# Decode attention on one core: results turned by fp32 transpositions, bias of both halves in one product

## The chip, the core and the metric

One core of one Trainium2 chip. The time is device microseconds of one execution, read off the chip. Each execution also has a profile with a span, from the first to the last instruction that is recorded; the time is about 2 us longer than the span. Kernels are compared with runs of the kernel before made on the same chip in the same session. Ratios are the mean time of one kernel's fast runs over the mean of the other's fast runs of the same rounds, so they are not quite the ratio of the medians quoted here. In the lines of the profile PE is TensorE, PEld its weight loads, DVE VectorE, ACT ScalarE, POOL GpSimd and SP SyncE, which issues the loads; a q behind such a name is that engine's sequencer, and L237 is line 237 of the kernel.

## The reference, cut to what matters

```python
# x: (2, 1, 448); k_cache, v_cache: (2, 8, 32768, 256), the last W = 4096 positions are used
xn = layernorm(x)
q  = xn @ wq                                   # 16 heads of 256; 2 query heads share a key head
p  = softmax(q @ k.T * 256**-0.5)              # over 4096 positions
A  = (p @ v).reshape(2, 1, 4096) @ wo
h  = xn @ w1 + b1                              # 448 -> 1792
B  = (h * tanh(softplus(h))) @ w2              # 1792 -> 448
return x + A + B
```

All inputs are bf16. The keys and values of the window alone are 2 x 2 x 8 x 4096 x 256 elements of 2 bytes, 67 MB, and every byte is used once.

## The kernel before

The eight key heads go round one after the other: a key load of 4 MB, a value load of 4 MB and a piece of the output weights, all on one DMA queue; VectorE transposes the keys, TensorE makes the scores, ScalarE their exponentials, VectorE transposes those, and TensorE multiplies them with the values. The first six key heads end like this: `values` leaves an 8 x 512 result (2 groups of keys x 4 rows of batch and head), ScalarE copies it, `turn_o` turns it so that the key dimension lies on the partitions and adds the two groups, `finish` scales it and keeps each partition's own head, `mix` multiplies with the output weights.

```python
def turn_o(i):
    o_sb = state.pop(("o", i))
    pq = ps_q.tile([P, NJ * BR], FP32, tag="q", name="q")          # NJ = 4, BR = 4
    ...
    for j in range(NJ):
        for u in range(NP):                                        # NP = 2 groups of keys
            nc.tensor.matmul(pqv[:, j, :],
                lhsT=o_sb[:, u, j, :, :]..., rhs=ident_f[0:NR, u * BR : (u + 1) * BR],
                start=(u == 0 and j == 0), stop=(u == NP - 1), ...)

def finish(i):       # o = pq * (1/sum);  o = o * own;  oT = o[head 0] + o[head 1]
    ...
def dense_in():
    for c in range(NF):                                            # NF = 7
        for s in range(NS):                                        # NS = 7
            nc.tensor.matmul(hT_ps[:, c, :, :], lhsT=w1_v[:, s, c, :], rhs=xs[:, s, :, :],
                             start=(s == 0), stop=False, ...)
        for x in range(NX):                                        # NX = 2 halves of the layer
            nc.tensor.matmul(hT_ps[:, c, x, :], lhsT=b1_v[:, x, c, :], rhs=ones[:, :], ...)
```

The last two key heads take another way (`values_fixed`): their result comes out turned already, and sixteen small products with the output weights close the program.

The softmax here doesn't subtract the row's maximum and nothing guards it: scores larger than these inputs give would overflow.

## Time and profile before

| | before |
|---|---|
| time, median of 3 runs | 190.53 us (190.34 to 190.56) |
| span of the profiled run | 188.1 us (time 190.5) |
| TensorE, VectorE, ScalarE busy | 148.5, 106.8, 45.3 us |
| DMA | 77.66 MB, 96.7% of the span |
| last packet of an input, from the packet records | 184.20 us |
| store of the result issued | 185.88 us |

### The profile page before, as it was taken

The numbers are of one execution on the slowest core, as the hardware profiler recorded it, in microseconds if no ns is written. First come the engines' busy times: TensorE is split into PE (matmuls) and PEld (weight loads), VectorE is DVE, ScalarE is ACT, GpSimd is POOL, SyncE is SP. The second block draws the span as 40 slices with busy tenths as digits, with TensorE's granted clock in tenths as the row PEclk, the third lists the DMA queues.
The fourth block names the chain that finished last, engine by engine and source line by source line (L and its number), as shares of the span: only waits on it lengthen the run. The fifth ranks groups of instructions, "written<-read, shape, count | busy, mean of one in ns | idle before, by whom it ended". The sixth has DMA issues, their size and how long they took to land.

```text
span 188.1 us, 2516 instructions
## 1 busy us (share of the span) xinstructions
PE 148.5 (79%) x993; PEld 73.3 (39%) x993; DVE 106.8 (57%) x144; ACT 45.3 (24%) x148; POOL 16.4 (9%) x74
## 2 busy tenths in 40 slices
PE   0493099904989999978995989958995989999782
PEld 0141033901334454425342624334442534355771
DVE  6505497049671994089704991099407984985201
ACT  3005015200062225123322224032402242234001
POOL 7001500300003001200030003000110000000000
PEclk9999559965899999999999999999999999999955
DMA  6999899999999999999999999999999999999990
GB/s 223 422 470 446 378 441 428 439 442 446 432 446 439 427 407 414 432 432 405 473 430 439 439 432 425 418 432 421 440 439 439 400 429 432 456 432 390 425 367 17
DMA packets 5028, 77.81 MB, mean 414 GB/s; under 512 B 533, under 2 KB 1049, under 8 KB 2330
## 3 DMA queue, kind: packets, MB, share of 16 engines
q1 hardware_dynamic: 5012, 77.66, 96.7%
q8 instruction: 7, 0.11, 0.2%
q14 instruction: 3, 0.02, 0.0%
q10 hardware_dynamic: 6, 0.01, 0.0%
HBM read 77.67 MB, written 0.00 MB: 413 GB/s over the span
## 4 chain that ended last, share of the span: by engine, by line
DMA 67%; DVE 21%; PE 7%; SPq 1%; issue 1%; ACT 1%; ACTq 0%; DVEq 0%
DMA k<-in_A_k_cache_dram 57%; DVE kt L404 17%; DMA v<-in_A_v_cache_dram 10%; PE o L477 4%; DVE pT L442 3%; PE sc L416 3%; SPq L373 1%; ACT p L430 1%; PE psA L237 0%; SPq L114 0%; DVE sums L451 0%; DVE osum L536 0%; DVE oTm L543 0%; PE q L559 0%; ACTq L663 0%
## 5 line engine op out<-in xcount | busy, mean ns | idle before, releaser
L404 DVE STREAM_TRANSPOSE kt<-k 128x2048 f32<-128x2048 f32 x32 | 73.1, 2289 | 52.7 <-DMA k<-in_A_k_cache_dram 52.7
L416 PE MATMUL sc<-kt,qdiag 128*128 128x512 bf16 x256 | 62.5, 389 | 17.4 <-DVE kt L404 16.7
L430 ACT ACTIVATE p<-sc,off 128x256 bf16<-128x256 f32 x64 | 33.0, 543 | 70.7 <-PE sc L416 70.1
L416 PEld LDWEIGHTS <-qdiag 128*128 128x128 bf16 x256 | 23.0, 97 | 52.8 <-issue 20.5
L477 PE MATMUL o<-v,pT 128*8 128x512 bf16 x192 | 42.5, 379 | 0.0
L477 PEld LDWEIGHTS <-pT 128*8 128x8 bf16 x192 | 17.2, 92 | 22.4
L442 DVE STREAM_TRANSPOSE pT<-p 128x512 bf16<-128x512 bf16 x32 | 21.8, 682 | 5.5 <-ACT p L430 5.5
L289 POOL COPY qdiag<-qt 32x16 bf16<-32x16 bf16 x64 | 12.9, 247 | 120.2 <-PE sc L416 104.6
L486 ACT COPY o_sb<-o 8x512 f32<-8x512 f32 x12 | 6.3, 572 | 36.3 <-PE o L477 36.3
L516 PEld LDWEIGHTS q<-ident_f,o_sb 8*128 8x128 f32 x96 | 11.1, 186 | 2.5 <-issue 2.5
L430 ACT ACTIVATION_READ_ACCUMULATOR p<-sc,off 128x1 f32 x64 | 11.7, 182 | 0.0
L516 PE MATMUL q<-ident_f,o_sb 8*128 8x4 f32 x96 | 11.7, 249 | 0.0
L220 PE MATMUL psE<-v,act_bf 128*2 128x448 bf16 x14 | 4.8, 528 | 6.8 <-DVE act_bf L354 6.8
L269 PE MATMUL q_ps<-v,xq 128*128 128x512 bf16 x28 | 7.8, 446 | 2.5 <-DMA v<-in_A_wq_dram 2.5
L559 PE MATMUL q<-pT,v 128*128 128x4 bf16 x256 | 7.9, 169 | 1.5 <-DMA v<-in_A_v_cache_dram 1.3
L559 PEld LDWEIGHTS <-v 128*128 128x128 bf16 x256 | 7.5, 100 | 2.3 <-DMA v<-in_A_v_cache_dram 1.8
L220 PE MATMUL psE<-wo,oTm 128*2 128x448 bf16 x24 | 5.5, 352 | 2.9 <-DVE oTm L543 2.9
L269 PEld LDWEIGHTS <-xq 128*128 128x128 bf16 x28 | 3.1, 112 | 7.1 <-DVE xq L260 2.5
L279 DVE CAST q_sb<-q_ps 128x512 bf16<-128x512 f32 x2 | 1.3, 686 | 7.7 <-PE q_ps L269 7.7
L220 PEld LDWEIGHTS <-act_bf 128*2 128x2 bf16 x14 | 1.5, 116 | 9.8 <-DVE act_bf L354 6.9
L220 PEld LDWEIGHTS <-oTm 128*2 128x2 bf16 x24 | 1.5, 82 | 7.0 <-DVE oTm L543 4.9
L190 PE MATMUL xnT_ps<-ident,xn_bf 2*128 2x2 bf16 x7 | 0.5, 166 | 4.6 <-DVE xn_bf L138 4.6
(60 smaller groups left out, 44.2 us busy)
## 6 DMA issues: line engine op xcount, KB each, us to landing
k<-in_A_k_cache_dram SPq DMA_DIRECT2D x7, 4096.0 KB, 27.2
v<-in_A_v_cache_dram SPq DMA_DIRECT2D x7, 4096.0 KB, 29.4
k<-in_A_k_cache_dram SPq DMA_DIRECT2D x2, 2048.0 KB, 24.5
v<-in_B_w_dram SPq DMA_DIRECT2D x2, 1568.0 KB, 24.4
wo<-in_A_wo_dram SPq DMA_DIRECT2D x7, 448.0 KB, 30.4
v<-in_A_wq_dram SPq DMA_DIRECT2D x1, 2048.0 KB, 7.4
v<-in_A_v_cache_dram SPq DMA_DIRECT2D x1, 2048.0 KB, 15.4
v<-in_A_wq_dram SPq DMA_DIRECT2D x1, 1536.0 KB
```

The lines of the kernel that those rows point to most:

```text
L220: nc.tensor.matmul(psE[:], lhsT=lhsT, rhs=w, start=start, stop=stop, skip_group_check=True)
L269: nc.tensor.matmul(ps[u][:], lhsT=xq[:, s, :, :].rearrange("p j k -> p (j k)"), rhs=wq_sb[:, s, u * N5 : (u + 1) * N5], start=(s == 0), st ...
L289: nc.gpsimd.tensor_copy(out=tv[rows, :, e, j * Q : (j + 1) * Q : HS].rearrange("p n (b h) -> p n b h", b=Bsz), in_=qv[rows, :, h0 : h0 + r ...
L373: nc.sync.dma_start(out=t[:, cols], in_=src[:, :, cols])
L404: nc.vector.transpose(out=kt[:].bitcast(FP32), in_=k[:, half * TH * Dh : (half + 1) * TH * Dh].bitcast(FP32),)
L416: nc.tensor.matmul(psc[:], lhsT=qdiag[i % NW][:, n * NE + e, :], rhs=ktv[:, n, e, :, :], start=(n == 0 and e == 0), stop=(n == NB - 1 and ...
L430: nc.scalar.activation(out=pv[:, b, :, :], in_=sv[:, b, :, :], func=ACT.Exp, scale=scale, bias=off[:, b : b + 1], accum_out=state["rs", i] ...
L442: nc.vector.transpose(out=pT[:], in_=p_t.pop(s)[:])
L477: nc.tensor.matmul(po[:], lhsT=pT_t[i * NH + piece][:, uh * NP * Q : (uh + 1) * NP * Q : HS], rhs=v[:, u * NP : (u + 1) * NP, :].rearrange ...
L486: nc.scalar.copy(out=o_sb[:, u, :, :, :], in_=po[:, u * Dh : (u + 1) * Dh] .rearrange("r (m j) -> r j m", j=NJ) .unsqueeze(2) .to_broadcas ...
L516: nc.tensor.matmul(pqv[:, j, :], lhsT=o_sb[:, u, j, :, :].rearrange("r h m -> r (h m)"), rhs=ident_f[0:NR, u * BR : (u + 1) * BR], start=( ...
L559: nc.tensor.matmul(po[:, c, :], lhsT=vv[:, t, c, :], rhs=pTv[:, th, 0:Q:HS], start=(t == 0 and c == 0), stop=(t == T - 1), skip_group_chec ...
```

## The change

Its intent: fewer and cheaper TensorE instructions. An fp32 product of the kernel before shows as two records in the trace (96 for 48 products); the hope is that an fp32 transposition shows as one. So `turn_o` only transposes, and the two groups of keys and the two heads are added on VectorE afterwards. The VectorE sums need more on-chip memory; the bias in two rows instead of one takes 1.8 KB a partition less, and with it the bias of both halves becomes one product with a small identity.

```diff
-    b1_sb = consts.tile([1, F], BF16)
+    b1_sb = consts.tile([NX, HF], BF16)          # loaded as two rows
+    half = consts.tile([NX, NX, Bsz], BF16)      # copied from the identity
...
-            for x in range(NX):
-                nc.tensor.matmul(hT_ps[:, c, x, :], lhsT=b1_v[:, x, c, :], rhs=ones[:, :], ...)
+            nc.tensor.matmul(hT_ps[:, c, :, :]..., lhsT=b1_v[:, c, :], rhs=half[:]..., ...)
...
-        state["rec", i] = denominator(i)
+        rec = denominator(i)                     # and rec * own into state["rec", i], on VectorE
...
-                nc.tensor.matmul(pqv[:, j, :], lhsT=o_sb[:, u, j, :, :]...,
-                    rhs=ident_f[0:NR, u * BR : (u + 1) * BR], ...)
+                nc.tensor.transpose(pqv[:, j, u, :], o_sb[:, u, j, :, :]..., ident_f[0:NR, 0:NR])
...
-        o = pq * rec;  o = o * own;  oT = o[..., 0] + o[..., 1]         # three VectorE operations
+        for u in range(NP): o[:, :, u, :] = pqv[:, :, u, u * BR : (u + 1) * BR] * rec
+        oT = tensor_reduce(o over u and h)                               # three VectorE operations
```

More of the change, by code (lines that the diff above doesn't have):

```diff
@@ L100 @@
     nc.scalar.dma_start(out=x_bf[:, :], in_=A_x.flatten_outer_dims())
-    b1_sb = consts.tile([1, F], BF16)
-    nc.scalar.dma_start(out=b1_sb[:, :], in_=B_b1.rearrange("(o f) -> o f", o=1))
+    b1_sb = consts.tile([NX, HF], BF16)
+    nc.scalar.dma_start(out=b1_sb[:, :], in_=B_b1.rearrange("(x f) -> x f", x=NX))
     def v_tile():
@@ L212 @@
             )
-    ones = consts.tile([1, Bsz], BF16)
-    nc.vector.memset(ones[:], 1.0)
     psE = ps_a.tile([Bsz, D], FP32, name="psE")
@@ L296, in build_q @@
                 )
+    half = consts.tile([NX, NX, Bsz], BF16)
+    nc.vector.tensor_copy(
+        out=half[:], in_=ident[0:NX, 0:NX].unsqueeze(2).to_broadcast([NX, NX, Bsz])
+    )
     act_bf = consts.tile([P, NF, NX, Bsz], BF16)
@@ L317, in dense_in @@
         w1_v = dense.pop("w1").rearrange("p s (q c) -> p s c q", c=NF)
-        b1_v = b1_sb[:].rearrange("o (x q c) -> o x c q", x=NX, c=NF)
+        b1_v = b1_sb[:].rearrange("x (q c) -> x c q", c=NF)
         hT_ps = ps_m.tile([P, NF, NX, Bsz], FP32, tag="m", name="hT_ps")
@@ L329, in dense_in @@
                 )
-            for x in range(NX):
-                nc.tensor.matmul(
-                    hT_ps[:, c, x, :],
-                    lhsT=b1_v[:, x, c, :],
-                    rhs=ones[:, :],
-                    start=False,
-                    stop=True,
-                    skip_group_check=True,
-                )
+            nc.tensor.matmul(
+                hT_ps[:, c, :, :].rearrange("p x b -> p (x b)"),
+                lhsT=b1_v[:, c, :],
+                rhs=half[:].rearrange("o x b -> o (x b)"),
+                start=False,
+                stop=True,
+                skip_group_check=True,
+            )
         shape = [P, NF, NX, Bsz]
@@ L473, in values @@
         v = v_t.pop(i)
-        state["rec", i] = denominator(i)
+        rec = denominator(i)
+        state["rec", i] = small.tile([P, BR], FP32, tag="recm", name="recm")
+        nc.vector.tensor_tensor(
+            out=state["rec", i][:],
+            in0=rec[:],
+            in1=own[:].rearrange("p b h -> p (b h)"),
+            op=ALU.mult,
+        )
         for u in range(T // NP):
@@ L511, in turn_o @@
         o_sb = state.pop(("o", i))
-        pq = ps_q.tile([P, NJ * BR], FP32, tag="q", name="q")
-        pqv = pq[:].rearrange("p (j r) -> p j r", j=NJ)
+        pq = ps_q.tile([P, NJ * NP * NR], FP32, tag="q", name="q")
+        pqv = pq[:].rearrange("p (j u r) -> p j u r", j=NJ, u=NP)
         for j in range(NJ):
             for u in range(NP):
-                nc.tensor.matmul(
-                    pqv[:, j, :],
-                    lhsT=o_sb[:, u, j, :, :].rearrange("r h m -> r (h m)"),
-                    rhs=ident_f[0:NR, u * BR : (u + 1) * BR],
-                    start=(u == 0 and j == 0),
-                    stop=(u == NP - 1),
-                    skip_group_check=True,
+                nc.tensor.transpose(
+                    pqv[:, j, u, :],
+                    o_sb[:, u, j, :, :].rearrange("r h m -> r (h m)"),
+                    ident_f[0:NR, 0:NR],
                 )
@@ L528, in finish @@
         rec = state.pop(("rec", i))
-        o = small.tile([P, NJ, Bsz, rep], FP32, tag="osum", name="osum")
-        nc.vector.tensor_tensor(
-            out=o[:].rearrange("p j b h -> p j (b h)"),
-            in0=pqv,
-            in1=rec[:].unsqueeze(1).to_broadcast([P, NJ, BR]),
-            op=ALU.mult,
-        )
-        nc.vector.tensor_tensor(
-            out=o[:].rearrange("p j b h -> p j (b h)"),
-            in0=o[:].rearrange("p j b h -> p j (b h)"),
-            in1=own[:].rearrange("p b h -> p (b h)").unsqueeze(1).to_broadcast([P, NJ, BR]),
-            op=ALU.mult,
-        )
-        oT = small.tile([P, NJ, Bsz], BF16, tag="oTm", name="oTm")
-        nc.vector.tensor_tensor(
-            out=oT[:], in0=o[:, :, :, 0], in1=o[:, :, :, 1], op=ALU.add
-        )
+        o = small.tile([P, NJ, NP, BR], FP32, tag="osum", name="osum")
+        for u in range(NP):
+            nc.vector.tensor_tensor(
+                out=o[:, :, u, :],
+                in0=pqv[:, :, u, u * BR : (u + 1) * BR],
+                in1=rec[:].unsqueeze(1).to_broadcast([P, NJ, BR]),
+                op=ALU.mult,
+            )
+        oT = small.tile([P, NJ, Bsz], BF16, tag="oTm", name="oTm")
+        with nc.allow_low_precision("sums of fp32 factors, rounded once"):
+            nc.vector.tensor_reduce(
+                out=oT[:],
+                in_=o[:].rearrange("p j u (b h) -> p j b u h", b=Bsz),
+                axis=AXIS.XY,
+                op=ALU.add,
+            )
         state["oT", i] = oT
```

## The prediction

What no trace or run of this case shows of the hardware is cut from the recorded text, and the cuts are marked. Its sum: TensorE 142.0 us, VectorE 108.0 us and 0.0 us on the path that sets the end, so 190.5 us. A "pass" in it is one record of the trace, two for each fp32 product. In the third rival, that an idle stretch brings the clock down was the author's assumption, from one stretch in which it fell (idle from 37.9 to 44.8 us) beside one in which it did not (2.1 us); in the range, the allowance for another chip's rate was a guess.

> **What bounds the kernel now.** I read the page from the top: span and engines, the row of slices, the DMA queues, the chain. Then the queue's own waits, one-microsecond and longer windows, and the timeline of the end.
>
> ```profile
> span 188.1 us, 2516 instructions
> PE 148.5 (79%) x993; PEld 73.3 (39%) x993; DVE 106.8 (57%) x144; ACT 45.3 (24%) x148; POOL 16.4 (9%) x74
> ...
> DMA  6999899999999999999999999999999999999990
> ...
> q1 hardware_dynamic: 5012, 77.66, 96.7%
> ...
> DMA 67%; DVE 21%; PE 7%; SPq 1%; issue 1%; ACT 1%; ACTq 0%; DVEq 0%
> ```
>
> The reader is to see that no compute engine is near its span (TensorE 79%, VectorE 57%), while one DMA queue is at work for 96.7% of it, in every slice but the first and the last. 77.66 MB pass through it, and the change moves none of those bytes. The windows say how steadily:
>
> ```profile
> 0.00:4.00 4.00, 0.00 (x0) 0.00 (x0) 2.23 (x6) 1.58 (x2) 3.39 (x10) 1.00 0.60 193
> 4.00:60.00 56.00, 37.22 (x190) 17.38 (x191) 28.81 (x44) 11.17 (x36) 6.45 (x33) 0.82 1.02 435
> 60.00:120.00 60.00, 54.48 (x271) 25.50 (x270) 36.15 (x42) 16.01 (x54) 4.90 (x24) 1.00 1.00 430
> 120.00:180.00 60.00, 52.80 (x436) 27.23 (x434) 38.74 (x49) 16.03 (x54) 1.64 (x8) 0.99 1.00 426
> ```
>
> Columns: stretch, length, busy time and count of PE, PEld, DVE, ACT, POOL, the granted TensorE clock, DMA share, GB/s. The transfer rate is 435, 430 and 426 GB/s in three stretches in which TensorE's load differs much (37 of 56 us, then 54 of 60). The span is therefore a sum: 1.65 us of start-up, then bytes over rate, then the tail after the last byte.
>
> The chain of waits seems to say otherwise, because it gives VectorE 21%: each key load is "released" by the VectorE transposition that frees its buffer. So the second question is whether the queue ever runs dry. The queue's own waits:
>
> ```profile
> SPq L373 <- PE o L477: 53.8, 6, 11.1
> SPq L373 <- DVE kt L404: 50.2, 6, 10.2
> ...
> SPq L373 <- PE psE L220: 17.6, 1, 17.6
> ```
>
> The sequencer that issues loads does wait on TensorE and VectorE, for over 100 us. To see what that costs I added up the GB/s of 188 one-microsecond windows and set the sum against the megabytes issued so far. When a load is issued, this much is still queued ahead of it: 3.6 MB at the value load at 49.63 us (the one behind the 17.6 us wait), 5.7 to 7.7 MB at all loads from 55 to 143 us, and 3.6 MB at the last value load at 163.01 us. At 428 GB/s the smallest of these is 8.4 us of work, the usual one 17 us. So the waits are waits for a free buffer ahead of a full queue; they hold back no byte until a release comes more than 8 us later than today.
>
> The end:
>
> ```profile
> 164.89 18.50 DMA v<-in_A_v_cache_dram
> 183.40 0.05 issue
> 183.44 0.39 PE q L559 x8
> 183.83 0.02 issue
> 183.86 0.18 DVE oT L498
> ```
>
> The last bytes land at 183.40 us. What follows, 4.7 us, is eight value products, a scaling, sixteen products of the output projection, two copies and the store. All of it belongs to the last two key heads, which go through another routine (values times weights directly transposed) that the diff does not touch.
>
> [...] here, from 60 to 170 us, the one-microsecond windows with VectorE above 0.9 average 432 GB/s and those below 0.1 average 431. So fewer or more engine operations should not change the rate. [...] no fp32 transposition is in this trace, so its duration is the uncertain one below. [...] idle from 37.9 to 44.8 us the clock fell to 0.5, while the idle of 2.1 us before the score products at 144.7 us left it at 1.00.
>
> **The change part by part.**
>
> (1) Turning the results of six key heads (the fp32 products at L516). Now, for one head:
>
> ```profile
> 164.75 1.86 PEld L516 LDWEIGHTS q<-ident_f,o_sb 8*128 8x128 f32 x16 [0.42 <-issue]
> 164.76 1.94 PE L516 MATMUL q<-ident_f,o_sb 8*128 8x4 f32 x16
> ```
>
> Eight products are recorded as 16 (two passes each) and take 1.94 us, that is 0.117 us a pass once pipelined. After, eight transpositions of 8x128 with an identity of 8 columns. If each is one pass: 8 x 0.117 = 0.94 us plus the last one's 0.1, so about 1.0 us, 0.9 us less a head and 5.6 us less over six heads. If each still takes two passes: nothing saved. Nothing waits for TensorE's time there beyond a microsecond: in that head the next score products (L416) start at 166.63 us, and TensorE then runs on to the final value products.
>
> (2) VectorE's sums. Now a head has three operations, 0.135 + 0.176 + 0.167 = 0.48 us. After: a product of reciprocals with the head mask, on 128x4 (the row nearest to it, the mask product of 128x16, takes 0.176; I take 0.15), two products of 128x16 from PSUM (0.135 each at the least, 0.176 when waiting), and a reduction of 128x32 to 128x8 (the reduction of 128x8 takes 0.120, the sum 0.167; I take 0.2). Sum 0.15 + 0.31 + 0.20 = 0.66, that is 0.18 us more a head and about 1.1 us over six heads. These sit in VectorE's chain between the key transpositions, so each key load's issue moves about 0.2 us later, against 17 us of queued work: no effect on landing.
>
> (3) The bias of the dense layer. 14 products become 7; from the timeline a pair took 0.26 us, so seven pairs become seven singles and 0.9 us goes from TensorE around 33 to 38 us. The VectorE copy that consumes them (L341) starts only at 43.1 us, because it stands behind the next key transpositions on its engine, so the gain ends as idle time. The bias load becomes two rows of 1.8 KB in place of one of 3.5 KB; it has 30 us to land. A memset of 0.06 us becomes a small copy of some 0.14 us in the start, where the first projection waits for it and for the query weights alike: at most 0.1 us.
>
> Sum by engine: TensorE 148.5 - 5.6 - 0.9 = 142.0 us, VectorE 106.8 + 1.1 + 0.1 = 108.0 us, DMA bytes unchanged. On the path that sets the end, start-up plus bytes over rate plus tail: 0.0 us, give or take 0.1. So 190.5 us.
>
> **The rivals.** First: the buffers' releases matter after all, through TensorE. In the last part TensorE is busy without a break from 156 to 177 us, and the final value load at 163.01 us is released by its value products. If the queue were dry, 0.9 us less a head would shift that load, and the time would fall by 1 to 2 us (to about 189). Against it: 3.6 MB are queued at that moment, and the DMA share is 1.00 up to 180 us. The value products are also gated by VectorE's fourth key transposition (ending at 153.82, the scores at 153.96), not by the turned results.
>
> Second: the extra VectorE work lengthens the chain that the page prints. If a chain of "VectorE transposition, key load" really set the pace, 0.2 us a head over six heads would add 1.2 us (191.7). Against it is the same queue: a key load takes 25 to 29 us to land although 4 MB need only 9.8 us.
>
> Third: the clock. With less to do, TensorE idles longer[...]. The steady round is 20.4 us with 17.4 us of TensorE; at half clock for a whole round, the matrix products of 512 columns would take (from the 0.43 us spacing seen at clock 0.50) some 27 us, and TensorE would become the bound: 200 us or more if it stuck. Against it: the long idle stretch in a round waits for a key load, between value products and the first score products, and the freed time falls elsewhere, just behind those first score products, in pieces of about 1 us. A dip at the end, where the clock is 0.5 from 179 us already, changes nothing as the products there wait for data.
>
> Fourth: the transfers run at another rate because of a different chip or placement[...].
>
> **Range and chances.** The three runs of before span 0.22 us. To that I add 0.2 us for the start and the reordering and some for another chip's rate: 189.9 to 191.1 us holds it 8 times in 10. Two per cent is 3.8 us. A gain of that size would need DMA time to vanish, and no byte does: 1%. A loss needs the third rival or a start-up stall: 2%. The rest, 97%, is within 2%.
>
> **What would show it.** Right: the DMA queue again near 97% with 77.66 MB, about 430 GB/s in the three stretches, last value landing near 183.4 us and 4.7 us after it; L516's successor with 48 records in place of 96 and about 1.0 us a head; TensorE near 142 us and VectorE near 108 us. Wrong in a part: 96 records for the transpositions (two passes), or VectorE's new operations well above 0.66 us a head; neither would move the time. Wrong in the whole: a stretch in the steady part with a DMA share well under 1, a granted clock of 0.5 between 60 and 170 us, or a load landing later with TensorE or VectorE named as its releaser and nothing queued ahead.

## The result, and the profile after

The changed kernel takes 189.66 us (median of 6 runs, 189.53 to 190.00) against 190.55 us of before (6 runs, 190.34 to 190.63). The ratio of the fast runs is 0.9957 (95% interval 0.9944 to 0.9969). That is 0.9 us less: small, well inside the 2% band, but clear of the noise and below the range (189.9 to 191.1).

The page of the changed kernel, its lines for the span, the engines, the slices, the queue and the chain:

```profile
span 187.8 us, 2412 instructions
PE 141.0 (75%) x938; PEld 65.0 (35%) x938; DVE 108.6 (58%) x150; ACT 45.3 (24%) x148; POOL 16.3 (9%) x74
...
q1 hardware_dynamic: 5012, 77.66, 96.9%
...
DMA 66%; DVE 20%; PE 8%; SPq 2%; ACT 1%; issue 1%; ACTq 0%; DVEq 0%
```

TensorE does 7.5 us less, VectorE 1.8 us more, and the DMA queue the same bytes. The same three windows as before (columns as in the prediction):

```profile
4.00:60.00 56.00, 37.44 (x186) 17.20 (x187) 29.46 (x49) 11.46 (x37) 6.42 (x33) 0.85 1.01 434
60.00:120.00 60.00, 50.48 (x245) 21.33 (x244) 36.50 (x45) 16.02 (x54) 4.90 (x24) 1.00 1.00 430
120.00:180.00 60.00, 49.31 (x418) 23.39 (x416) 39.06 (x52) 16.03 (x54) 1.63 (x8) 0.98 1.00 427
```

434, 430 and 427 GB/s: the transfers run as they did. Added up microsecond by microsecond, the two kernels' bytes agree within 0.1 MB from 179 us on, and the last packet of an input lies at 184.20 us before and 184.26 us after. So none of the 0.9 us comes from ahead of the last byte. The turning of one head, in the timeline of the changed kernel:

```profile
165.06 0.57 PEld L523 LDWEIGHTS q<-ident_f,o_sb 8*128 8x128 f32 x8 [0.42 <-issue]
165.06 0.66 PE L523 MATMUL q<-ident_f,o_sb 8*128 8x8 f32 x8
```

One record for each transposition instead of two for each product, and 0.66 us instead of 1.94. The freed time went where the prediction said: into TensorE's waits. Its product and weight-load tracks together now wait 16.8 us for VectorE's sums (7.8 before).

What did change is the tail. First the chain of waits of the kernel before, from where the prediction broke off (start, length, what):

```profile
184.08 0.35 PE psA L237 x6
184.43 0.44 issue
184.86 0.49 PE psA L237 x10
185.35 0.23 ACT res L635
```

Sixteen like products: six, then a hole of 0.44 us labelled "issue" (the engine waits for nothing that the profile shows), then ten. There is a real wait in these sixteen, for the last weights, but it stands ahead of the ninth product, not of the seventh. The same place in the changed kernel, by weight loads (start, length, engine, ..., count):

```profile
184.15 0.18 PEld L234 LDWEIGHTS <-oT 128*2 128x2 bf16 x9 [0.35 <-DVE oT L505]
184.58 0.10 PEld L234 LDWEIGHTS <-oT 128*2 128x2 bf16 x7 [0.26 <-issue]
```

Here the pause stands where it belongs: nine weight loads and eight products go, the ninth product starts at 184.58, right after the last weights land at 184.54, as the chain of the changed kernel has it:

```profile
167.20 17.34 DMA wo<-in_A_wo_dram
184.54 0.04 issue
184.58 0.46 PE psA L234 x8
```

Before, even the seventh and the eighth product, whose weights had landed at 183.96 us, started only at 184.86. But the hole cost less than its length. The trace also records the sixteen completion signals of that load: the last of them came at 184.71 us before, 0.50 us behind the last packet, and at 184.54 us after, 0.27 us behind it. In the six traces without a hole in which the ninth product waits for that signal, it starts 0.04 to 0.05 us behind it. So before it could have started at about 184.75 us instead of 184.87, and the hole cost about 0.12 us there (an estimate from these figures; the store follows the start of the ninth product by 1.01 us in both kernels). From the last packet to the store it is 1.68 us before (185.88 - 184.20) and 1.33 us after (185.59 - 184.26). Of this 0.35 us the later signal is 0.23 us and the hole 0.12 us; what delayed the signal, no run tells. Since the last packet lies 0.06 us later in the changed kernel, the spans differ by 0.3 us. The rest of the 0.9 us is outside them: 190.5 - 188.1 = 2.4 us before, and in the six runs of the changed kernel 1.81 to 1.88 five times and 2.3 once.

### The profile page after: what moved, and what is told of

Its sections match the earlier page's. It is cut to its first block, busy times and chain, and to the rows that moved or that the text cites. A ratio compares the mean times of both kernels' runs of the same rounds, so it can differ in the third digit from the quotient of the medians.

```text
span 187.8 us, 2412 instructions
## 1 busy us (share of the span) xinstructions
PE 141.0 (75%) x938; PEld 65.0 (35%) x938; DVE 108.6 (58%) x150; ACT 45.3 (24%) x148; POOL 16.3 (9%) x74
## 3 DMA queue, kind: packets, MB, share of 16 engines
q1 hardware_dynamic: 5012, 77.66, 96.9%
## 4 chain that ended last, share of the span: by engine, by line
DMA 66%; DVE 20%; PE 8%; SPq 2%; ACT 1%; issue 1%; ACTq 0%; DVEq 0%
DMA k<-in_A_k_cache_dram 57%; DVE kt L404 16%; DMA wo<-in_A_wo_dram 9%; PE sc L416 4%; PE o L484 4%; DVE pT L442 3%; SPq L373 2%; ACT p L430 1%; PE psE L217 0%; SPq L114 0%; DVE sums L451 0%; SPq L398 0%; DVE oTm L544 0%; DVE recm L476 0%; PE psA L234 0%
## 5 line engine op out<-in xcount | busy, mean ns | idle before, releaser
L266 PE MATMUL q_ps<-v,xq 128*128 128x512 bf16 x28 | 8.7, 487 | 2.1 <-DVE xq L257 2.1
L523 PEld LDWEIGHTS q<-ident_f,o_sb 8*128 8x128 f32 x48 | 3.4, 136 | 2.5 <-issue 2.5
L276 ACT CAST q_sb<-q_ps 128x512 bf16<-128x512 f32 x2 | 1.1, 588 | 12.5 <-PE q_ps L266 12.5
```

The costliest lines, as they stand in the source:

```text
L266: nc.tensor.matmul(ps[u][:], lhsT=xq[:, s, :, :].rearrange("p j k -> p (j k)"), rhs=wq_sb[:, s, u * N5 : (u + 1) * N5], start=(s == 0), st ...
L523: nc.tensor.transpose(pqv[:, j, u, :], o_sb[:, u, j, :, :].rearrange("r h m -> r (h m)"), ident_f[0:NR, 0:NR],)
```

## The experiments

Twelve kernels, five rounds each, in three sets; the runs of before made with them have a median of 190.58, 190.51 and 190.58 us. In each set one or two of the eleven runs of before took 192.4 to 192.8 us; they are under the bound for the slow state and so are in the ratios, which is why I quote medians, and spans and times outside them for each run. Because of those slow runs the 95% interval of the ratio reaches 1 for five of the twelve kernels (`after_pad`, `before_pad24`, `after_pad55`, `turn_pad48`, `after_pad44`); what is said of them rests on medians and ranges. All twelve kernels gave the right result.

### First set: which half of the change, and is it the length of TensorE's program?

The trace of before has an 8 KB instruction fetch 2.1 us after its span, that of after has none. That made my first theory: the shorter program saves a fetch. Rivals: the saved work itself, or the other form of the bias load.

`bias_only`: the bias half of the diff on the kernel before, nothing else.

> The kernel before with the bias half of the change alone (14 fewer TensorE instructions, a two-row bias load, nothing else). Program-length theory (an instruction fetch of 8 KB that the trace of before shows 2.1 us after its span, and that of after lacks, is paid in the time): 189.7 to 190.0 us, no such late fetch, time less span near 1.9 us instead of 2.4. Work theory (the shorter turning of results on TensorE makes the gain): 190.5 us. Bias-load theory (the two-row load or the changed start makes it): 189.7 us.

`turn_only`: the other half on the kernel before.

```diff
 # the changed kernel with the bias as before, and, to fit:
-        o = small.tile([P, NJ, NP, BR], FP32, tag="osum", name="osum")
+        o = small.tile([P, NJ, NP, BR], FP32, tag="osum", name="osum", bufs=2)
```

> The turning half alone (transpositions and VectorE sums), bias as before; one small tile has two buffers instead of three because it does not fit otherwise. As many TensorE instructions in the program as before. Program-length theory: 190.2 to 190.5 us, the late fetch is there. Work theory: 189.7 us. Bias-load theory: 190.5 us.

`after_pad`: the changed kernel with seven products issued twice (the first of each group, which only overwrites itself).

```diff
-            for s in range(NS):
+            for s in (0, *range(NS)):
```

> The changed kernel with seven bias-layer products issued a second time (same result), so that TensorE's program has as many instructions as before: 14 more than after. Program-length theory: back to 190.2 to 190.5 us, the late fetch returns. Work theory and bias-load theory: 189.7 us.

`after_again`: the changed kernel as it is.

> The changed kernel once more, as the control of this set: 189.7 us against 190.5 us of before under every theory; if it is 190.2 or more, the 0.9 us was a matter of the chip or the load and no theory is needed.

| | time, median (range) | span, median | outside the span, six runs | last packet to store |
|---|---|---|---|---|
| before | 190.58 | 188.3 | 2.17 to 2.46 (eleven runs) | 1.68 us |
| bias_only | 189.99 (189.86 to 190.18) | 188.05 | 1.79 to 1.88, one 2.18 | 1.55 us |
| turn_only | 189.90 (189.64 to 190.32) | 187.8 | four 1.82 to 1.89, two 2.3 | 1.34 us |
| after_pad | 190.09 (189.70 to 190.47) | 187.95 | two 1.8, four 2.29 to 2.37 | 1.32 us |
| after_again | 189.88 (189.58 to 190.43) | 187.9 | three 1.8 to 1.9, three 2.2 to 2.3 | 1.32 us |

(The last column is from each one's trace.) Ratios: 0.9960, 0.9956, 0.9963, 0.9957. So the 0.9 us is not a matter of the chip, but either half alone brings 0.6 to 0.7 us of it, and they do not add. The theory of program length had `bias_only` right (189.7 to 190.0 us, no late fetch), but it fell: the padded kernel, though its trace has the late fetch again, came to 190.09 us and not back to 190.2 or more; the turning half, which I had counted as no shorter, was as fast as the whole, and the late fetch shows in the unchanged `after_again` (2.07 us after its span). The theory of the bias load fell with the turning half, which keeps the old load and is as fast. The work theory fell in that the bias half, which saves 0.4 us of TensorE's time (seven groups of products at 0.61 us instead of 0.66) at a place where nothing waits for it, brought most of the gain.

What remained was the hole in the tail. The weight loads of `bias_only`:

```profile
184.14 0.18 PEld L234 LDWEIGHTS <-oT 128*2 128x2 bf16 x9 [0.35 <-DVE oT L498]
184.59 0.09 PEld L234 LDWEIGHTS <-oT 128*2 128x2 bf16 x4 [0.28 <-issue]
184.94 0.09 PEld L234 LDWEIGHTS <-oT 128*2 128x2 bf16 x3 [0.26 <-issue]
```

Behind the regular pause at the ninth there is a second one, after 13 of the 16: seven products later than in before, and seven products (each a weight load and a product, so 14 instructions) are what the bias half removes. Counted from the last product backwards, the hole lies 20 instructions from the end in before and 6 in `bias_only`. In both, the same kind of hole lies 256 instructions earlier: 276 from the end in before (after 8 of 64 products at 178.48 us), 262 in `bias_only` (after 15). The four kernels with the turning half, 96 recorded instructions shorter or more, have none in the last 32.

So the second theory: TensorE's instruction stream is cut every 256 instructions, the distance between the two holes of one kernel (276 - 20 in before, 262 - 6 in `bias_only`), and at a cut TensorE can stand still (0.44 us in before). That it waits there for instructions is a guess that no run shows; the page's queue list has seven packets of 16 KB of the kind "instruction" in before, after, `bias_only` and `turn_only`, and no more than that. Where no hole is found, the place of a cut is computed from the 256 and the instructions that were added. The line of the page (queue, kind, packets, MB, share):

```profile
q8 instruction: 7, 0.11, 0.2%
```

### Second set: move the cut, not the work

All four kernels add needless products at the start of the bias layer (they overwrite themselves, the result is the same), after 33 us and before 50 us, far from the tail:

```diff
-            for s in range(NS):
+            for s in [0] * k + list(range(NS)):    # k for each of the 7 groups, n in all
```

`before_pad24`: n = 24 in the kernel before.

> The kernel before with 24 needless products (48 TensorE instructions) in the bias layer, same result. Boundary theory (TensorE's instruction stream is cut every 256 instructions; in before a cut lies 20 instructions from the end of the products, inside the last 16 products after the last byte, and costs some 0.35 us there; in the first set the cut lay at 6 in the bias half, and at none in the last 32 of the others): the cut moves to 68 from the end, where TensorE waits for data anyway, so no unexplained gap in the last 16 products, store issued 1.33 us after the last packet instead of 1.68, span about 187.9, although TensorE does more work than in before. Work theory (less TensorE work makes the gain): span 188.2 or more, store 1.68 us after the last packet.

`after_pad55`: n = 55 in the changed kernel.

> The changed kernel with 55 needless products, which makes up exactly the 110 TensorE instructions that the change removed. Boundary theory: the cut is again 20 from the end; TensorE stalls after six of the last 16 products until about 184.85, store 1.6 to 1.7 us after the last packet, span 188.2 as before, 0.35 us over the changed kernel. Work theory: about 4 us of TensorE work come back near 40 us, not in the tail; the span stays at 187.85 or, if any work counts, goes back to 188.2 too, but without a stall after six products.

`after_pad51`: n = 51.

> The changed kernel with 51 needless products, four fewer than the one above. Boundary theory: the stall moves by four products, to ten of the last 16 done (12 instructions from the end), store 1.5 to 1.7 us after the last packet, span 188.0 to 188.2. Work theory: no stall at a definite place, span as with 55.

`after_pad79`: n = 79.

> The changed kernel with 79 needless products, more than the one with 55: as many TensorE instructions as the padded before. Boundary theory: cut at 68 from the end, no stall in the last 16 products, store 1.33 us after the last packet, span 187.85: more work and yet 0.35 us faster than with 55. Work theory: as slow as with 55 or slower. On the time outside the span (2.3 us in all runs of before, 1.8 or 2.3 in the others) I have no theory that predicts a kernel; whichever run shows 2.3 should have the 8 KB instruction fetch 2.07 us after its span in its trace, and the others not.

| | cut, instructions from the end | time, median (range) | span, median | outside the span | hole found after |
|---|---|---|---|---|---|
| before_pad24 | 68 | 189.69 (189.61 to 191.48) | 187.85 | four 1.81 to 1.85, 2.18, 2.32 | none (trace of the 191.48 run) |
| after_pad55 | 20 | 190.28 (190.20 to 190.79) | 187.95 | 2.30 to 2.44 in all six | 6 of 16 |
| after_pad51 | 12 | 189.80 (189.69 to 190.04) | 188.0 | 1.79 to 1.89 in all six | 10 of 16 |
| after_pad79 | 68 | 190.15 (189.75 to 190.22) | 187.9 | two 1.8, four 2.2 to 2.4 | none |

Ratios: 0.9967 (with the one run of 191.48), 0.9983, 0.9953, 0.9965. The first row decides against the work theory: the kernel before, with 24 products more and not one line of the change, runs in 189.69 us, as fast as the changed kernel; five of its six runs (189.61 to 190.32) lie below all eleven of before in that set (190.38 and more). And the hole stands where it was foretold. `after_pad55`, then `after_pad51`:

```profile
184.15 0.10 PEld L234 LDWEIGHTS <-oT 128*2 128x2 bf16 x6 [0.34 <-DVE oT L505]
184.55 0.18 PEld L234 LDWEIGHTS <-oT 128*2 128x2 bf16 x10 [0.31 <-issue]
```

```profile
184.03 0.18 PEld L234 LDWEIGHTS <-oT 128*2 128x2 bf16 x9 [0.35 <-DVE oT L505]
184.45 0.08 PEld L234 LDWEIGHTS <-oT 128*2 128x2 bf16 x1 [0.24 <-issue]
184.82 0.10 PEld L234 LDWEIGHTS <-oT 128*2 128x2 bf16 x6 [0.29 <-issue]
```

Six and ten weight loads, then TensorE stands still without a semaphore to wait for. In `after_pad51` that costs: from the last packet to the store 1.65 us. In `after_pad55` it does not (1.33 us): the hole was over by 184.55 us, just when the last weights landed (184.56), for which the ninth product waits anyhow. There the expected 188.2 us of span was a miss; the time went up all the same, to 190.28 us, because all six runs have 2.3 us outside the span. So the outside part also seemed to follow the cut, against what I had written beforehand (no theory): at 20 always 2.3, at 12 always 1.8, elsewhere mixed.

The profiled run of `before_pad24` is the one of 191.48 us, and shows something else. In windows (columns as before), and the score products of one stretch:

```profile
144.00:158.00 14.00, 13.25 (x46) 6.60 (x47) 10.58 (x14) 2.20 (x9) 0.00 (x0) 0.63 0.99 420
```

```profile
144.75 3.13 PE sc L416 x8
147.88 3.50 PE q L516 x16
```

The granted clock fell to 0.5 from 145.3 to 155.5 us. Eight score products took 3.13 us instead of 1.90, the value products ended at 166.8 us instead of 163.0, the last value load was issued 3.8 us later, and the store only at 187.03 us. The late load did not land late: the last packet lies at 184.32 us. It was TensorE that came late. This is the prediction's third rival, here with a cost. Nothing above rests on that trace: the times and spans of the other five runs (spans 187.8 to 188.0) carry the row.

### Third set: the same places with the other arithmetic

Is it the place of the cut, or the arithmetic around it? `before_pad124` is the kernel before with n = 124, 248 instructions more, which moves the cut from 20 to 12.

> The kernel before with 124 needless products in the bias layer: 248 instructions more, so a cut of TensorE's stream (every 256) lies 12 instructions from the end of the products instead of 20. Boundary theory, by the case with the same place (the changed kernel with 51 needless products): unexplained gap after ten of the last 16 products, span 187.9 to 188.2, time outside the span 1.8 us in nearly all runs (2.3 in before), 189.8 to 190.0 us in all. Work theory: over 9 us more TensorE work than in before, so 190.5 us or more. If the outside time belongs to the old arithmetic and not to the cut's place: 2.3 us outside, 190.4.

`turn_pad48`: the turning half alone with n = 48.

> The turning half alone with 48 needless products: cut again 20 from the end, as in before. Boundary theory: the gap after six of the last 16 products is back, outside time 2.3 us in nearly all runs (1.8 or 2.3 without the padding), 190.2 to 190.5 us against 189.9. Work theory: 189.9.

`after_pad44`: the changed kernel with n = 44.

> The changed kernel with 44 needless products: cut 2 instructions behind the end of the products, in the stretch that nothing waits for. Boundary theory: no gap in the last 16 products, span 187.85. If the outside time goes with the cut's place as it seems (1.8 in all runs with the cut at 12 or 6), 1.8 outside in most runs and 189.65 us, the best of all versions; if only a cut at certain places matters, 1.8 or 2.3 mixed and 189.9.

`after_pad59`: the changed kernel with n = 59.

> The changed kernel with 59 needless products: cut 28 from the end. Boundary theory: a gap after two of the last 16 products, short where it ends before the last weights land anyway (0 to 0.35 us on the span of 187.85); outside time 2.3 as with the cut at 20 if it goes with the place, mixed otherwise. Work theory: no gap there.

| | cut | time, median (range) | span, median | outside the span | last packet to store | hole found after |
|---|---|---|---|---|---|---|
| before_pad124 | 12 | 190.02 (189.84 to 190.14) | 188.2 | 1.81 to 1.87 in all six | 1.68 us | 10 of 16 |
| turn_pad48 | 20 | 190.27 (190.05 to 190.45) | 188.0 | 2.15 to 2.42 in all six | 1.35 us | 6 of 16 |
| after_pad44 | 2 behind the end | 189.85 (189.72 to 191.44) | 188.05 | five 1.79 to 1.84, one 3.04 | 1.38 us | none |
| after_pad59 | 28 | 189.97 (189.81 to 190.32) | 188.1 | 1.81 to 1.89 in all six | 1.62 us | 2 of 16 |

Ratios: 0.9952, 0.9965, 0.9955, 0.9952. Two of the foretold places, `before_pad124` and `after_pad59`:

```profile
184.13 0.18 PEld L237 LDWEIGHTS <-oT 128*2 128x2 bf16 x9 [0.35 <-DVE oT L498]
184.58 0.08 PEld L237 LDWEIGHTS <-oT 128*2 128x2 bf16 x1 [0.28 <-issue]
185.00 0.10 PEld L237 LDWEIGHTS <-oT 128*2 128x2 bf16 x6 [0.34 <-issue]
```

```profile
184.27 0.08 PEld L234 LDWEIGHTS <-oT 128*2 128x2 bf16 x2 [0.35 <-DVE oT L505]
184.89 0.27 PEld L234 LDWEIGHTS <-oT 128*2 128x2 bf16 x14 [0.54 <-issue]
```

All four places came out as computed. What the hole cost, estimated as above from the signal of the last weights and the store, is 0.34 us in `before_pad124`, 0.30 in `after_pad51`, 0.21 in `bias_only`, 0.15 in `after_pad59`, 0.12 in before, and nothing in `after_pad55` and `turn_pad48`, where it ends when the signal comes (184.77 us in the latter, the rest starts at 184.81).

The outside part: over all sets the fast runs of before and the six of each of `after_pad55` and `turn_pad48`, cut at 20 in each, have 2.14 us or more outside the span without exception (leaving out before's four runs of over 192 us, of which three have 1.84 to 1.86 and one 2.35). The five kernels with the cut at 28, 12, 12, 6 and 2 behind the end have 1.79 to 1.89 in 28 of 30 runs. Cuts further off give a mixture. So the outside part goes with the place of the cut under either arithmetic, and `before_pad124`, with 7.1 us more TensorE time (155.6 against 148.5; the "over 9" expected was too much), is 0.56 us faster than before. One thing the runs do not separate: the cut was only ever moved by the length of the stream. The three kernels with the cut at 20 are equally long; at 12 two lengths, 256 instructions apart, agree. So it may be the cut or where the stream ends within its last 256 instructions that decides the outside part. That at 28 it would be 2.3 was a miss: being near the end is not enough.

In all 14 traces, the late 8 KB fetch (2.1 to 2.3 us after the span) is there in the seven whose run has over 2.1 us outside and absent in the seven under 1.9. What that fetch waits on, and why the cut's place decides it, no run tells; the profile ends there.

`after_pad44` was meant to be the best version: no hole and 1.8 us outside. At 189.85 us it is level with the changed kernel (189.66 and 189.88 in its two sets), so I claim no version that beats both. Its span of 188.05 us also missed the 187.85 expected: in this set the kernel without a hole is no shorter than the three with one (188.0 to 188.2), so here the spans do not confirm what the traces give for the hole.

**What stays open.** With the cut at one place, the changed arithmetic is still 0.2 to 0.3 us ahead: at 20, 190.28 and 190.27 against 190.55 us; at 12, 189.80 against 190.02. With no cut in the tail there is no such lead (189.69 for the padded before, 189.66 and 189.88 for the changed one). At 20 this is in line with the hole, which cost some 0.1 us in the trace of before and nothing in the other two. At 12 it stays open: the hole cost about the same in both, and in the changed kernel's trace the last packet lay 0.15 us earlier (184.10 against 184.25), on another chip. In the five traces where the hole is exposed TensorE resumes 2.2 to 2.4 us after the start of the last 16 KB instruction packet (before: 182.69 to 184.86). In `after_pad55` that packet starts at 182.27 us, which by the same 2.2 to 2.4 us would put the end of the hole at 184.5 to 184.7 (an estimate), about where the weights land. Why the packet starts earlier there was not tried. Nor is it shown that TensorE waits for this packet: it starts between 182.27 and 182.69 us in twelve of the fourteen traces, wherever the cut lies.

## Why the prediction was right or wrong

**The bound, the transfers, the rate: right.** DMA at 96.9%, the same bytes, 434, 430 and 427 GB/s, last packet within 0.06 us. The queue was never dry; even the first value load, issued at 17.49 us instead of 15.94 in the changed kernel's trace, left the bytes landed by 60 us within 0.1 MB. The strongest check came by chance: in `before_pad24` the last value load was issued 3.8 us later, and the last packet still lay at 184.32 us. One reading was wrong: 183.40 us is where the last values land, not the last bytes; the last weights' packets end at 184.20 us, and eight of the sixteen products wait for them.

**The turning (1): right in kind, mis-sized.** 48 records in place of 96 as foretold, but 0.66 us a head and not 1.0, so 7.7 us less over six heads and not 5.6. TensorE came to 141.0 us (foretold 142.0); part of what was saved went back into the query projection, 8.7 us instead of 7.8.

**VectorE's sums (2): right.** 0.16 for the masked reciprocal, 0.22 for the two products together and 0.18 for the reduction, 0.56 us a head against 0.66 foretold, and none of it on the path. VectorE came to 108.6 us (foretold 108.0); part of the excess is at the start, where the first conversion (L119) is recorded with 2.7 us instead of 1.0. It has the one or the other length in the traces of several kernels, and the first projection then starts later without any load landing later.

**The bias (3): right in kind, mis-sized, and the gain did end as idle time.** It was 0.4 us and not 0.9: a group takes 0.61 us instead of 0.66. And its 14 instructions moved the cut of the stream by 14, which the part did not consider.

**The step that failed** is the sum: "On the path that sets the end, start-up plus bytes over rate plus tail: 0.0 us, give or take 0.1", and under it the sentence on the tail, that all of it "belongs to the last two key heads, which go through another routine ... that the diff does not touch". The code of the tail was untouched; its place in TensorE's stream of instructions was not. Two terms were missing from the sum: waits in the tail, and 0.5 us outside the span. The tail became 0.35 us shorter from the last packet to the store; by the estimate above about 0.12 us of it is the hole in the last sixteen products and 0.23 us an earlier signal of the last weights, whose cause stays open. In other traces the hole alone cost up to 0.34 us. The hole could be seen: the chain of waits holds the line "184.43 0.44 issue", three pieces after the prediction stopped quoting, at a place where no wait belongs. The outside part was there as 190.5 against 188.1, 2.4 us that the sum never named.

**The rivals.** The first foresaw a gain, by a value load that starts earlier; the trace shows no load that lands earlier, so the gain is not its. The second did not come. The third did not come in the changed kernel's first profile, but it did in its second: in `after_again` the clock was 0.5 from 84.0 to 90.8 us and from 125.0 to 131.8 us, which the prediction named as a sign of being wrong in the whole. The page's row shows it (tenths of full speed in 40 slices of 4.7 us):

```profile
PEclk9999558855699999995899999985999999999755
```

Six of the fourteen traces have such dips between 60 and 170 us, 3.4 to 10.2 us long (mean clock of the six runs 0.868 to 0.878, of the other eight 0.912 to 0.928). In five of them the last packet lies at 184.20 to 184.48 us all the same; only the long dip near the end in `before_pad24` shows a cost. So the clock did drop, and the full queue hid it. What brings it down, the traces do not show: in before it fell at 38.65 us, 0.7 us after the last product, and stayed at 1.00 over 2.37 us without a product (from 101.54 us) and 2.12 us (to 144.71 us); in `before_pad24`, after 2.13 us without one up to 144.75 us, it fell at 145.3 us. The fourth did not come (434, 430 and 427 GB/s against 435, 430 and 426).

**The range** of 189.9 to 191.1 us was built from run-to-run scatter, the start and a guess for another chip's rate. The chance of 97% for "within 2%" was right.

## What to carry to other kernels

When a kernel is bound by transfers, count the tail behind the last byte instruction by instruction, and question every "issue" hole in it that stands where no semaphore is waited for. A change of a few tenths of a per cent need not come from the work that was removed: here the kernel before with 24 needless products, and so with the cut of TensorE's stream elsewhere, ran in 189.69 us against 190.51. So before crediting an edit, pad the old kernel with harmless instructions and see whether it gets as fast. And set the time against the span: what lay outside it moved too, between 1.8 and 2.5 us in nearly all runs here.
